# A new order of steps, with newly assigned buffers, for a gated linear attention and mixing kernel on one core

## The chip, the core and the metric

The kernel runs on one core of a Trainium2 chip. A core has five engines that each work through a list of instructions in order: TensorE (PE in the profile; its weight loads are PEld), VectorE (DVE), ScalarE (ACT), GpSimd (POOL) and SyncE (SP), which here issues all DMA transfers. They wait for each other by semaphores. The metric is the device time of one execution in microseconds (us).

## The reference, cut to what matters

```python
# q, k, v, f_logit: 4 batches, 8 heads, 768 tokens, 48 wide, fp32
f = sigmoid(f_logit)
for t in range(S):                      # per batch and head
    state = f[t][:, None] * state + outer(k[t], v[t])
    y[t] = q[t] @ state
x = y as (batch, token, 8 * 48 = 384)
theta = x @ w_theta                     # 384 x 384
zr, zi = x * cos(theta), x * sin(theta)
u = x + w_tok_r @ zr + w_tok_i @ zi     # 768 x 768 over tokens
out = u + relu(u @ w_ch)                # 384 x 384
```

## The kernel before

The tokens of a batch are cut into 6 chunks of 128; the four batches give chunks 0 to 23. For each chunk the attention part runs in chunk form, and then the mixing part. Half a batch (384 tokens) is a group; there are 8 groups, and each has 3 blocks of 128 channels. The work is written as steps with short names, and a table of strings, ORDER, lists 1169 steps; the main function walks through it, and each engine gets its instructions in that order. A suffix puts a step's operation on another engine (/A ACT, /D DVE, /P POOL). A second table, PLACES, says for each allocation of a buffer kind which of its buffers it takes. No scheduler changes the order afterwards: every engine works in order, so an instruction that waits holds all that stand behind it on its engine.

The steps of a chunk, in the order of their dependence, with the line on which their instructions are recorded:

- lf, lk, lq, lv: loads of f, k, q, v (SP, L560 and L565). lw: load of a part of a weight (L205). Each kind has 3 buffers per tag.
- gc (clamp, L272, DVE or POOL), go (two activations, L277 and L278, ACT), gs (scan over the tokens, L282, DVE), ge (p and f exponentials, L289 and L290, ACT), gq (q times p, L297, DVE or POOL), gk (k times f, L302, DVE), gp (copy of the chunk's last p into pes, L293, POOL). There is one buffer for p.
- ke (transposes of k into psk, L352, PE), kt (copy ktok out of psk, L179), up (state sums, L367, PE), sa (mid, L373 or L375, DVE), st (new state, L379, DVE), sm (its fading, L383, DVE or POOL).
- sc (scores, L338, PE), ma (mask, L344, DVE), qs (old state times q, L398, PE), ou (scores times v, L406, PE), xc (copy x out, L179), xt (transposes of x into pxt, L416, PE), xs (copy into ut, L179).
- th (angles, pth, L447, PE: from chunk 6 on in three products of an upper and a lower part, xh and xl), tn (rounding, L452 or L454), se (settle, L458, DVE), ab (fold, L463 on ACT or L465 on DVE), tr (two sines, L470 and L471, ACT), ro (x times sines gives z, L480, DVE), zh and zl (upper and lower part of z, L179 and L487).
- f0, f1, f2 (products over the tokens into pm, L503, PE: one step for each chunk of a group and each block of channels; for the first batch in full fp32, after it in three products of parts), v (adds pm to u, L507, DVE), uh and ul (parts of u, L179 and L514), c (channel product pch, L521, PE), cv (relu and sum, L535, DVE), so (store, SP).
- d1 to d5, e4, e5: the weights arrive as 64-bit words and are decoded on DVE (L218, L228, L229: raw, then value) and ACT (L223), and split into parts (L179, L253).

sc, up, qs and ou write into two double PSUM tiles, wide0 and wide1; psk, pxt, pth, pm and pch share four PSUM banks of the tag "b". ACT needs one table of functions for the gate's exponentials and logarithms and another for the sines; going from one to the other is an ACT_TABLE_LOAD.

Of the kernel before, what the change touches and what calls it, by code (L numbers as in the profile page):

```python
# [17 lines left out]
B, H, S, D = 4, 8, 768, 48  # L18
DM = H * D
P = 128  # L20
# [34 lines left out]


PLACES = {
    "a": "0110110101001010110101010101010101010101010101010",
    "b": ("012301230120123023300300002121123222230230203120310202001031023333312312023011203100000023"
        "1030303030032123123211120303031"),  # L60
    "f": "012012012012012012012012",
    "k": "012012012012012012012012",
    "q": "012012012012012012012012",
# [3 lines left out]
    "ut": "01201201",  # L67
    "v": "012012012012012012012012",
    "w": "010101010101010101010101",
    "wp": "0123456789abcdefghijklmno013245687cd",  # L70
    "x": "012012012012012012012012",
    "z": "0123450123412342342350421350421350421",
}
ORDER = (
# [37 lines left out]
)  # L112


# [636 lines left out]
```

## Time and profile before

| | us |
|---|---|
| three runs | 335.24, 335.41, 335.74 |
| their median | 335.41 |
| the profiled execution | 335.43 |
| its span from the first to the last instruction | 333.7 |
| PE busy | 319.3 (96%) |
| PE weight loads busy | 283.8 (85%) |
| DVE busy | 243.7 (73%) |
| ACT busy | 191.2 (57%) |
| POOL busy | 112.6 (34%) |

A profile gives for each instruction its engine, its line, when it began and how long it took. Matmuls overlap, so the time of one in a row of matmuls is longer than the distance between two starts; the distances are what adds up. An engine's idle time is put down to the instruction that released it. Of the chain of work that ended last, 89% lies on PE.

### The profile page before, as it was taken

What the parts mean: (1) busy time and instruction counts of PE and PEld (TensorE: products, weight loads), DVE (VectorE), ACT (ScalarE), POOL (GpSimd) and SP (SyncE); (2) the same over time, 40 slices, a digit from 0 to 9 for tenths busy, and PEclk for the clock granted to TensorE, in tenths of its full rate; (3) what the DMA queues carried; (4) which work ended last, traced back from release to release, by engine and by line L of the source; (5) the groups of instructions that cost most, each with busy time, mean ns of one, the idle gap of its engine ahead of it and who ended that gap; (6) DMA issues with size and microseconds to landing.
All of it is one profiled execution on the core that took longest, in us unless ns stands there. A gap on an engine that the chain in (4) does not pass through costs nothing.

```text
span 333.7 us, 10043 instructions
## 1 busy us (share of the span) xinstructions
PE 319.3 (96%) x4342; PEld 283.8 (85%) x4342; DVE 243.7 (73%) x397; ACT 191.2 (57%) x321; POOL 112.6 (34%) x109
## 2 busy tenths in 40 slices
PE   6599999999999999999999999999999999999992
PEld 6485667567676789999999999999999999999992
DVE  6999999999999899968659786764427677430031
ACT  6789977687696699847368254952806252300010
POOL 2452173318100146265371248153800521102110
PEclk9758999999999999999999999999999999999998
DMA  6988979858660464250404343250122102000022
GB/s 240 401 272 281 292 247 294 287 180 311 255 200 17 155 224 110 83 166 9 136 10 152 128 165 110 92 177 0 33 93 74 35 2 74 0 2 0 0 74 78
DMA packets 21619, 45.54 MB, mean 136 GB/s; under 512 B 2369, under 2 KB 5441, under 8 KB 21569
## 3 DMA queue, kind: packets, MB, share of 16 engines
q1 hardware_dynamic: 21568, 44.84, 40.6%
q8 instruction: 36, 0.59, 0.7%
q14 instruction: 15, 0.11, 0.1%
HBM read 40.11 MB, written 4.72 MB: 134 GB/s over the span
## 4 chain that ended last, share of the span: by engine, by line
PE 89%; DVE 3%; DMA 3%; ACT 2%; issue 1%; SPq 0%; DVEq 0%; ACTq 0%
PE pm L503 48%; PE pth L447 12%; PE pch L521 11%; PE wide L406 4%; PE wide L398 3%; PE wide L338 3%; PE pxt L416 3%; PE psk L352 3%; PE wide L367 2%; DMA q<-in_q_dram 2%; DVE f L282 1%; DMA f<-in_f_dram 1%; DVE q L297 0%; DVE k L302 0%; ACT L470 0%
## 5 line engine op out<-in xcount | busy, mean ns | idle before, releaser
L503 PE MATMUL pm<-wp,z 128*128 128x384 f32 x648 | 117.1, 336 | 0.0
L503 PEld LDWEIGHTS pm<-wp,z 128*128 128x128 f32 x648 | 112.4, 188 | 0.0
L503 PE MATMUL pm<-value,z 128*128 128x384 f32 x144 | 49.3, 488 | 0.4 <-DVE z L480 0.4
L503 PEld LDWEIGHTS pm<-value,z 128*128 128x128 f32 x144 | 26.3, 190 | 16.1 <-PE wide L406 0.5
L521 PE MATMUL pch<-uhl,wch 128*128 128x384 f32 x216 | 39.9, 338 | 0.0
L521 PEld LDWEIGHTS pch<-uhl,wch 128*128 128x128 f32 x216 | 37.5, 188 | 0.3
L507 DVE TENSOR_TENSOR ut<-pm,ut 128x384 f32<-128x384 f32 x24 | 13.1, 552 | 30.2 <-PE pm L503 30.2
L293 POOL COPY pes<-p 128x4 f32<-128x4 f32 x24 | 10.6, 440 | 71.0 <-ACT p L289 70.9
L179 ACT CAST uhl<-ut 128x384 fp32r<-128x384 f32 x18 | 9.2, 510 | 41.5 <-DVE ut L507 41.5
L282 DVE TENSOR_TENSOR_SCAN f<-carry,f 128x512 f32<-128x512 f32 x24 | 29.2, 1228 | 0.5 <-ACT f L278 0.5
L438 POOL TENSOR_TENSOR xl<-ut,xh 128x384 fp32r<-128x384 f32 x13 | 13.6, 1050 | 46.2 <-DVE xh L179 29.2
L289 ACT ACTIVATE p<-f 128x512 f32<-128x512 f32 x24 | 15.1, 628 | 22.3 <-DVE f L282 21.2
L514 POOL TENSOR_TENSOR uhl<-ut,uhl 128x384 fp32r<-128x384 f32 x13 | 13.5, 1046 | 37.0 <-DVE uhl L179 18.6
L272 POOL TENSOR_SCALAR f<-f 128x512 f32<-128x512 f32 x14 | 24.1, 1722 | 1.5 <-DMA f<-in_f_dram 1.5
L535 DVE SCALAR_TENSOR_TENSOR ut<-pch,ut 128x384 f32<-128x384 f32 x24 | 13.0, 552 | 14.6 <-PE pch L521 14.4
L447 PE MATMUL pth<-wth,xh 128*128 128x384 f32 x108 | 23.1, 348 | 0.0
L487 POOL TENSOR_TENSOR z<-w,z 128x768 fp32r<-128x768 f32 x9 | 16.8, 1863 | 17.1 <-ACT z L179 9.6
L406 PEld LDWEIGHTS wide<-v,sc 64*64 64x64 f32 x768 | 15.0, 140 | 8.8 <-DVE sc L344 3.6
L302 DVE SCALAR_TENSOR_TENSOR k<-f,k 128x512 f32<-128x512 f32 x24 | 19.3, 805 | 3.8 <-ACT f L290 3.8
L480 DVE TENSOR_TENSOR w<-w,x 128x768 f32<-128x768 f32 x18 | 18.2, 1013 | 4.0 <-ACT w L471 4.0
L458 DVE SCALAR_TENSOR_TENSOR w<-w,pth 128x384 f32<-128x384 f32 x24 | 13.2, 548 | 10.4 <-ACT w L452 10.3
L406 PE MATMUL wide<-v,sc 64*64 64x48 f32 x768 | 18.0, 231 | 2.3 <-DVE sc L344 2.3
(88 smaller groups left out, 609.1 us busy)
## 6 DMA issues: line engine op xcount, KB each, us to landing
v<-in_v_dram SPq DMA_DIRECT2D x24, 384.0 KB, 4.4
f<-in_f_dram SPq DMA_DIRECT2D x24, 256.0 KB, 4.1
k<-in_k_dram SPq DMA_DIRECT2D x24, 256.0 KB, 3.8
q<-in_q_dram SPq DMA_DIRECT2D x24, 256.0 KB, 3.9
raw<-in_w_r_dram SPq DMA_DIRECT2D x12, 384.0 KB, 4.8
raw<-in_w_i_dram SPq DMA_DIRECT2D x12, 384.0 KB, 5.4
out_dram<-ut SPq DMA_DIRECT2D x21, 192.0 KB, 1.9
raw<-in_w_theta_dram SPq DMA_DIRECT2D x3, 384.0 KB, 6.5
```

Of the source, the lines that this page charges most:

```text
L272: on(nc.vector).tensor_scalar(ft, ft, F_MIN, None, op0=ALU.max)
L282: nc.vector.tensor_tensor_scan(fl, carry[:, pairs(h)].rearrange("p n t -> p (n t)"), fl, 0.0, ALU.mult, ALU.add)
L289: nc.scalar.activation(ps_[m][:, pairs(h)], ft, AF.Exp, scale=-1.0)
L302: nc.vector.scalar_tensor_tensor(kt, loaded["f", m][:, pairs(h)], E_TOP, kt, op0=ALU.min, op1=ALU.mult)
L406: nc.tensor.matmul(out[HALF[t], j, p, :], scs[m][HALF[a], j, p, :], v2[HALF[a], t, p, :], start=(t == 0 and m % NC == 0 and p == 0), stop= ...
L438: on(nc.vector).tensor_tensor(xls[m], src, xhs[m], op=ALU.subtract)
L447: nc.tensor.matmul(pths[m], l, r, start=(n == 0), stop=(n == len(ms) - 1))
L480: nc.vector.tensor_tensor(zs[m] if full else w, w, xs[m].unsqueeze(1).to_broadcast([P, 2, DM]), op=ALU.mult)
L487: on(nc.vector).tensor_tensor(zs[m][:, 0], ws[m], zs[m][:, 1], op=ALU.subtract)
L503: nc.tensor.matmul(pms[g, d], l, r, start=(s == 0 and i == 0), stop=(s == NC - 1 and i == len(ms) - 1))
L514: on(nc.vector).tensor_tensor(us[g, d][:, 0], uts[g][:, d, :], us[g, d][:, 1], op=ALU.subtract)
L521: nc.tensor.matmul(pcs[g, d], l, r, start=(es[0] == 0 and n == 0), stop=(es[-1] == KD - 1 and n == len(ms) - 1))
```

## The change

The first 125 of the 1169 steps keep their order; all others come in a new one. Some steps move to another engine, and PLACES changes for the tags a (the double PSUM tiles), b (the PSUM banks), wp and z. No function is changed. Of the two tables this is the start of what changes:

```diff
-    "a": "0110110101001010110101010101010101010101010101010",
+    "a": "0110110011010101001001010101010101010101010101010",
-    "xt go d3 gs th lw gc ge gp tn se lv gq qs gk sc up ma lq d1 xs go gs sm/P ab/A th ge gq ke kt lk gp ou sa",
+    "xt go d3 gs th lw gc ge gp tn se lv gq qs gk sc up ma lq d1 xs go gs sm/P ab/A th ou ke ge tn sa xc d2",
```

By the tables, these numbers of steps move between engines: clamps gc on POOL 14 to 12, on DVE 10 to 12; gq on POOL 9 to 7; sm on POOL 11 to 16; copies kt on DVE 5 to 9; casts uh on DVE 6 to 13 and ul on POOL 13 to 9; zh on DVE 9 to 7; d5 on POOL 7 to 4. The switches of ACT's table, counted in the order, are 22 before and 26 now.

On PE, around the output step of chunk 7, where the attention steps of chunks 7 and 8 stand. In a row, the names give the tile with the number of its chunk or group, and the last columns the shape. Before:

```order
L503 MATMUL pm11_1139<-value9_1120,z0_624 128x384 x2
L352 MATMUL psk9_1173<-ident_70,k9_1022 128x112 x4
L406 MATMUL wide0_88<-v7_907,sc7_1178 64x48 x16
L338 MATMUL wide1_89<-q8_1010,k8_880 64x64 x16
L367 MATMUL wide1_89<-v9_1157,ktok9_1214 48x48 x16
L398 MATMUL wide0_88<-st7_1002,q8_1010 64x48 x2
```

Now:

```order
L503 MATMUL pm01_684<-value7_930,z4_1059 128x384 x2
L406 MATMUL wide1_89<-v7_780,sc7_1135 64x48 x16
L367 MATMUL wide0_88<-v8_1015,ktok8_1116 48x48 x16
L416 MATMUL pxt6_1183<-ident_70,x6_1048 128x128 x3
L503 MATMUL pm10_1187<-value8_990,z0_629 128x384 x2
L352 MATMUL psk9_1201<-ident_70,k9_1056 128x112 x4
L503 MATMUL pm10_1187<-value9_1052,z0_629 128x384 x2
L447 MATMUL pth6_1218<-wth1_85,xh6_1206 128x384 x3
L447 MATMUL pth6_1218<-wth0_84,xh6_1206 128x384 x3
L447 MATMUL pth6_1218<-wth1_85,xl6_1216 128x384 x3
L338 MATMUL wide0_88<-q8_1064,k8_883 64x64 x16
L398 MATMUL wide1_89<-st7_1045,q8_1064 64x48 x2
```

The output, scores, state and old-state steps stood in one block; now the output and a state step are one block, and the scores and the old state another, with transposes, products and angles between them.

On DVE, from the last common row (the scan of chunk 6) to the first z. Before:

```order
L282 SCALAR_TENSOR_TENSOR f6_392<-carry_67,f6_392 128x512
L297 TENSOR_TENSOR q5_504<-q5_504,p5_518 128x512
L375 TENSOR_TENSOR mid3_548<-wide0_88,st2_371 128x192
L379 TENSOR_TENSOR st3_550<-wide0_88,mid3_548 128x192
L383 TENSOR_TENSOR st3_550<-st3_550,pes_83 128x192
L302 SCALAR_TENSOR_TENSOR k5_529<-f5_300,k5_529 128x512
L228 SCALAR_TENSOR_TENSOR raw3_439<-raw3_439 128x768
L229 SCALAR_TENSOR_TENSOR value3_506<-raw3_439 128x768
L344 TENSOR_TENSOR sc3_620<-wide0_88,causal_75 128x512
L480 TENSOR_TENSOR z0_624<-w0_447,x0_282 128x768
```

Now:

```order
L282 SCALAR_TENSOR_TENSOR f6_392<-carry_67,f6_392 128x512
L375 TENSOR_TENSOR mid3_544<-wide0_88,st2_371 128x192
L458 SCALAR_TENSOR_TENSOR w1_542<-w1_542,pth1_514 128x384
L179 COPY ktok4_592<-psk4_534 128x384
L379 TENSOR_TENSOR st3_594<-wide0_88,mid3_544 128x192
L302 SCALAR_TENSOR_TENSOR k5_567<-f5_300,k5_567 128x512
L344 TENSOR_TENSOR sc3_622<-wide1_89,causal_75 128x512
L179 COPY ktok5_625<-psk5_617 64x384
L179 COPY ut0_390<-pxt2_613 128x3x128
L480 TENSOR_TENSOR z0_629<-w0_447,x0_282 128x768
```

The q scaling went to POOL, the decoding of value 3 behind z, and three copies and a settle step came in front of it.

On DVE, before the join that makes value 11. Before:

```order
L218 TENSOR_SCALAR raw12_1305<-raw12_1305 128x768
L302 SCALAR_TENSOR_TENSOR k10_1275<-f10_1056,k10_1275 128x512
L228 SCALAR_TENSOR_TENSOR raw11_1278<-raw11_1278 128x768
L229 SCALAR_TENSOR_TENSOR value11_1281<-raw11_1278 128x768
L282 SCALAR_TENSOR_TENSOR f11_1161<-carry_67,f11_1161 128x512
```

Now:

```order
L282 SCALAR_TENSOR_TENSOR f10_964<-carry_67,f10_964 128x512
L179 CAST uhl01_1291<-ut0_390 128x384
L218 TENSOR_SCALAR raw12_1212<-raw12_1212 128x768
L282 SCALAR_TENSOR_TENSOR f11_1120<-carry_67,f11_1120 128x512
L228 SCALAR_TENSOR_TENSOR raw11_1124<-raw11_1124 128x768
L229 SCALAR_TENSOR_TENSOR value11_1231<-raw11_1124 128x768
```

The scan of chunk 11 stood behind the join and now stands in front of it.

## Rows read from the trace of the kernel before

**Rows 1.** Stretches: from:to, length, busy time per engine (instructions), clock, DMA.
```profile
40.00:112.00 72.00, 71.97 (x1034) 48.91 (x1033) 70.43 (x109) 55.86 (x94) 23.33 (x21) 1.00 0.68 229
112.00:200.00 88.00, 87.97 (x1298) 84.77 (x1297) 71.73 (x119) 57.32 (x95) 39.52 (x33) 1.00 0.36 114
```

**Rows 2.** Waits of PE: engine, waiting line, released by, total, times, longest.
```profile
PE pxt L416 <- ACT x L179: 0.6, 1, 0.6
```

**Rows 3.** Timeline of PE: start, length, operation, count; angles, products, attention.
```profile
145.24 1.20 PE L447 MATMUL pth<-wth,xh 128*128 128x384 f32 x6
146.28 0.68 PE L447 MATMUL pth<-wth,xl 128*128 128x384 f32 x3
146.80 8.49 PE L503 MATMUL pm<-wp,z 128*128 128x384 f32 x48
...
260.33 1.20 PE L447 MATMUL pth<-wth,xh 128*128 128x384 f32 x6
...
261.98 0.72 PE L406 MATMUL wide<-v,sc 64*64 64x48 f32 x32
262.48 0.69 PE L338 MATMUL wide<-q,k 48*64 48x64 f32 x32
...
277.23 0.72 PE L406 MATMUL wide<-v,sc 64*64 64x48 f32 x32
277.88 1.31 PE L447 MATMUL pth<-wth,xh 128*128 128x384 f32 x6
```

**Rows 4.** Timeline of PE at a late angles step; chain of waits: start, length, what.
```profile
96.67 1.52 PE L447 MATMUL pth<-wth,xh 128*128 128x384 f32 x6
98.03 0.69 PE L447 MATMUL pth<-wth,xl 128*128 128x384 f32 x3
...
42.70 1.95 PE pth L447 x6
...
80.90 1.29 PE pm L503 x4
```

**Rows 5.** Timeline of DVE, 31 to 40 us, and of PE at the first products.
```profile
31.72 1.22 DVE L282 TENSOR_TENSOR_SCAN f<-carry,f 128x512 f32<-128x512 f32 x1
32.85 0.67 DVE L297 TENSOR_TENSOR q<-q,p 128x512 f32<-128x512 f32 x1
33.44 0.35 DVE L375 TENSOR_TENSOR mid<-wide,st 128x192 f32<-128x192 f32 x1
...
36.96 0.68 DVE L344 TENSOR_TENSOR sc<-wide,causal 128x512 f32<-128x512 f32 x1
37.76 0.96 DVE L480 TENSOR_TENSOR z<-w,x 128x768 f32<-128x768 f32 x1
...
38.87 1.53 PE L503 MATMUL pm<-value,z 128*128 128x384 f32 x4 [0.41 <-DVE z L480]
```

**Rows 6.** Groups by form: line, engine, operation, shapes, count, busy us, mean ns.
```profile
L179 DVE COPY ktok<-psk 128x384 f32<-128x384 f32 x4 | 2.2, 549 | 1.3 <-PE psk L352 1.3
L272 DVE TENSOR_SCALAR f<-f 128x512 f32<-128x512 f32 x10 | 4.2, 415 | 1.0 <-DMA f<-in_f_dram 1.0
L179 DVE CAST uhl<-ut 128x384 fp32r<-128x384 f32 x6 | 2.1, 353 | 0.0
L470 ACT ACT_TABLE_LOAD x11 | 14.1, 1283 | 0.2
L272 POOL TENSOR_SCALAR f<-f 128x512 f32<-128x512 f32 x14 | 24.1, 1722 | 1.5 <-DMA f<-in_f_dram 1.5
```

**Rows 7.** Timeline of PE and DVE at value 11, and PE's first channel step.
```profile
86.57 4.19 PE L503 MATMUL pm<-value,z 128*128 128x384 f32 x12
...
86.90 0.96 DVE L229 SCALAR_TENSOR_TENSOR value<-raw 128x768 int32<-128x768 int32 x1
...
111.48 1.85 PE L521 MATMUL pch<-uhl,wch 128*128 128x384 f32 x8
```

**Rows 8.** Operations on raw: count, shortest, median and longest ns, first and last.
```profile
L229 DVE SCALAR_TENSOR_TENSOR value<-raw x14: 558/959/1692, 14.5 to 96.7; 128x768 int32<-128x768 int32 x13, 128x384 int32<-128x384 int32 x1
```

More of the change, by code (lines that the diff above doesn't have):

```diff
@@ L57 @@
 PLACES = {
-    "a": "0110110101001010110101010101010101010101010101010",
-    "b": ("012301230120123023300300002121123222230230203120310202001031023333312312023011203100000023"
-        "1030303030032123123211120303031"),
+    "a": "0110110011010101001001010101010101010101010101010",
+    "b": ("012301230123021313133131120100131311201201021231321313132030120020001023012310120221122201"
+          "0310112122221231013010032103210"),
     "f": "012012012012012012012012",
@@ L69 @@
     "w": "010101010101010101010101",
-    "wp": "0123456789abcdefghijklmno013245687cd",
+    "wp": "0123456789abcdefghijklmno012354679bd",
     "x": "012012012012012012012012",
-    "z": "0123450123412342342350421350421350421",
+    "z": "0123450123401240140154032154032154032",
 }
```

66 rows, old and new, of the table ORDER are left out of this document.

## The prediction

> **What bounds the kernel now.** I first read the stretches with each engine's busy time [rows 1]. From 40 to 112 us TensorE (PE) is busy 71.97 of 72.00 us and VectorE (DVE) 70.43, so both are full; from 112 to 200 us PE still has 87.97 of 88.00, while DVE has fallen to 71.73 and ScalarE (ACT) to 57.32. The granted clock is 1.00 in both. PE is therefore the bound from about 40 us to the end, and up to about 112 us DVE, which makes most of PE's operands, is a second bound that runs level with it. A new order cannot change what PE computes: both orders hold the same PE steps. It can change three things: the time between two PE steps, the times at which PE waits, and the work left after the last matmul.
>
> The waits of PE that the profile names after the common start are short: 0.6 us for ACT's copy of x [rows 2] and 0.41 us for the first z [rows 5]. Less visible are three places where the angles' second half follows late: 98.03 - 96.67 = 1.36 us where the undisturbed run takes 146.28 - 145.24 = 1.04 us [rows 3, 4], so 0.3 us each. Together some 2 us in 300 can be won from waits, and no more than that.
>
> **The switch between matmul kinds.** The attention's four kinds (L338, L367, L398, L406) use 48 or 64 rows of the array, the others 112 or 128. The undisturbed nine matmuls of an angles step take 146.80 - 145.24 = 1.56 us to the start of a products step and 261.98 - 260.33 = 1.65 us to the start of an attention step: 0.09 us for going in. An L406 step takes 262.48 - 261.98 = 0.50 us to the next attention step and 277.88 - 277.23 = 0.65 us to an angles step: 0.15 us for coming out [rows 3]. So each block of attention steps costs 0.24 us, whatever its length. Counted in the PE order, the kernel before has 30 such blocks and the new one 35: the new order often cuts "ou sc up qs" in two or three (the first excerpt). That is 5 x 0.24 = 1.2 us on PE, which nothing covers, since PE is full. I take 1.2; a block that falls into one of PE's waits would cost nothing, so 0.7 to 1.2.
>
> **The start, 31 to 40 us.** PE's rows are the same up to the second angles step, DVE's up to the scan that starts at 31.72 and ends at 32.94 [rows 5]. Before, the q scaling (0.67) came next, then mid, and z began at 37.76, its table load and sines being late on ACT; the first products step began at 38.87 after an idle of 0.41. Now mid stands right behind the scan: done at 33.3, so the old-state step, which PE reaches at about 32.4, waits some 0.8 us there. After it I follow DVE's new rows (second excerpt) with the times of rows 5 and 6 (settle, ktok and ut take a ktok copy's 0.55, st is priced like mid, k like q): 0.55, 0.55, 0.35, 0.67, 0.68, 0.55, 0.55, and z 0.96, each some 0.08 less since they overlap. That puts ut at 36.8 and z at 37.7; the third angles step starts at 36.9, lasts 1.95 [rows 4], and the first products step starts at 38.9 with one more score step (0.5) behind it, thus about 0.4 us ahead of before. The table load now comes on ACT before the p and f exponentials, a gain for z, paid with another load right behind.
>
> **The stretch in which DVE feeds PE, 40 to 112 us.** The tight place of before is the join of value 11: DVE's L229 ends at 86.90 + 0.96 = 87.86, and PE's run of twelve records from 86.57 comes to it after four records of value 10, 1.29 us [rows 4], at 87.86 [rows 7]: no reserve at all. Against the common scan, DVE has in the new order, before that same join, two more ktok copies (2 x 0.55), a cast of uhl (0.35), three more clamps (3 x 0.415), one more scan (1.22), one more L454 (a PSUM operand of the same size as ktok's: 0.55) and one more fold (priced like mid, 0.35), together 4.8; and fewer: a q (0.67), a k (0.67), a mask (0.68) and three short operations of 192 columns (3 x 0.35), together 3.1 [rows 5, 6]. DVE has 1.7 us more to do. PE has before it one more products step (1.29 [rows 4]) and a block (0.24), less a key transpose and a state step (0.4 each, 86.57 and the run before): 0.7 us more. If DVE lost as much time in the new order as in the old, PE would come 1.0 us late there. What DVE lost: from 32.94 to 87.86 are 54.9 us, where its 81 operations, each at the median time from start to start of its form, add up to some 50.1, so 4.8 us, of which six operations account for 2.7 by taking far longer than their usual time (L229 up to 1.692 against 0.959 [rows 8]); the rest are its own waits. I take 0.7 less in the new order: 0.4 from the start, where z and the next mask no longer wait, and 0.3 because GpSimd (POOL) has there seven or eight long operations (clamps of 1.72 [rows 6] and q) instead of nine. This leaves 1.0 - 0.7 = +0.3 us. It swallows the 0.4 us of the start, which is inside it and not added. Bounds: -0.4 (DVE never late, PE keeps the gain of the start) to +2.0 (DVE loses 1.0 more than before).
>
> **The rest.** ACT has 26 table loads instead of 22 (11 of each kind), 4 x 1.283 = 5.1 us more [rows 6]; ACT is busy 55.86 of 72 us in the first stretch and 57.32 of 88 in the second [rows 1], and that room hides them. Without that cover a load would cost its 1.28 us. Operations moved from POOL to DVE late in the program (casts, splits) fall where DVE has 16 us free in 88: nothing. Loads on the DMA queue: I compared for each k and v the PE step that frees its buffer, with the stores queued ahead, and the PE step that uses it; the shortest distance is about 5 us before and 7 after by the step times above, so nothing either way. A PSUM bank is taken again one products or split step (six matmuls, 1.04 as in rows 3) after its last use at five places, before at one. The copy in between takes 0.55 [rows 6], so it fits if its engine is free; I take 0 and keep 0 to 1.5 us for the range. The end is alike: the last PE steps are six channel steps, then three additions and one store, and the splits that they need are made 1 us or more ahead.
>
> **The sum.** The profiled execution took 335.43 us, the median of the three runs is 335.41, so it stands for them. 335.43 + 1.2 + 0.3 = 336.9 us, 0.45% slower. A difference of 0.2%, 0.67 us, is about the least that a measurement of this kernel can tell from none.
>
> **Rivals.** (1) *PE keeps ahead of DVE's lateness.* If DVE is in time throughout, the start's gain of 0.4 stays: 335.43 + 1.2 - 0.4 = 336.2, with 0.7 for the blocks 335.7: within 0.2%, mostly. It speaks for it that DVE loses least where it begins without waits; against it, that the reserve of before was nil at value 11. (2) *The waits go and outweigh the blocks: faster.* All of the 0.6, the 0.41 and the three times 0.3 would be won, 1.9, and 0.4 at the start is partly the same; with blocks at 0.7 to 1.2 it gives 334.2 to 334.8. It decides from the point at which more than 1.9 us of waiting is gone. Its mechanism is that DVE is less often held up by POOL: the stretch's nine long POOL operations become seven or eight and stand elsewhere, so in the best case none of the six lengthened DVE operations (2.7 us) recurs. For it: L229's two lengths [rows 8]. Against: POOL is still full of work in the stretch, and before the common scan nothing changes. [...] (3) *Waits in order pile up later.* With PSUM banks taken again after 1.04 us and chains of copy, split and sine spread over engines that work in order, each late copy holds PE: some five to eight waits of 0.3 to 0.5 us more, 338.4 to 340. For it: five close reuses instead of one. Against it: after 112 us every engine but PE has room.
>
> **How the numbers follow.** Forecast as summed (336.2 to 338.2): 0.47. Rival 1, no change or just slower: 0.22. Rival 2, faster: 0.17. Rival 3: 0.14. The range should leave out about 2 in 10: the lower end takes in rival 1 and the edge of rival 2, 335.0; the upper end takes the bounds of DVE's lateness (1.2 + 2.0) and part of rival 3, 338.8. Faster by over 0.2%, below 334.7: 0.17. Within 0.2%, 334.7 to 336.1: 0.21. Slower, above 336.1: 0.62.
>
> **What would show it.** In the new profile, nine matmuls of angles to an attention step should again take 0.09 more, and leaving one 0.15 more, at 35 places. The first products step should start near 38.9 with the old-state step waiting for mid before it. At value 11 and at the first z of chunk 4 PE should wait for DVE, and the first channel step should start about 0.6 us earlier than the 111.48 of before [rows 7], with one products step less behind it, if I am right about DVE's pace; 1 us earlier or more means rival 1 or 2. After 112 us PE's waits should be as short as now; if they add up to over 1 us, rival 3. I am wrong altogether if DVE's lengthened operations vanish or double.

## The result, and the profile after

| | us | runs | ratio to the kernel before (95% interval) |
|---|---|---|---|
| before | 335.74 | 335.24 to 335.95, five | |
| after | 337.95 | 336.76 to 340.19, five | 1.0079 (1.0054 to 1.0105) |
| after, once more | 338.60 | 336.79 to 342.24, eight | 1.0092 (1.0058 to 1.0127) |

The new order is slower by 2.2 us. That is on the side I had forecast and inside my range, 1 us above the 336.9. But its runs lie over more than 3 us where those of before lie over 0.7, and no term of my sum spreads like that. The longest of the eight runs of the repetition is a slow one that its ratio leaves out. The profiled execution is the 340.19 one, so 4.8 us above the profiled one of before.

From its page, these are the busy line, the granted clock in 40 slices, and the head of the chain that ended last (before: PE 319.3, DVE 243.7, ACT 191.2, POOL 112.6):

```profile
PE 322.6 (95%) x4342; PEld 284.8 (84%) x4342; DVE 257.3 (76%) x411; ACT 194.1 (57%) x318; POOL 106.7 (32%) x102
...
PEclk9959899999999999999999999999999999999998
...
PE 77%; DVE 14%; issue 3%; DMA 3%; ACT 1%; SPq 0%; DVEq 0%; ACTq 0%
```

DVE has 13.6 us more to do and POOL 5.9 less, as the moved steps said. The new thing is "issue 3%" in the chain: time in which the engine waited for nothing that the profile shows. The waits of PE (engine and line, what it waited for, us in total, times, longest), over the whole span, say where; this answers [rows 2]:

```profile
PE wide L406 <- DVE sc L344: 2.9, 3, 2.0
PE wide L338 <- issue: 2.2, 1, 2.2
PE wide L398 <- DVE mid L375: 0.6, 1, 0.6
```

One wait of 2.2 us that no semaphore ends. PE's timeline (start, length, operation, count, idle before) around it, which answers the PE row of [rows 5]:

```profile
35.67 0.34 PE L338 MATMUL wide<-q,k 48*64 48x64 f32 x8
38.22 0.58 PE L338 MATMUL wide<-q,k 48*64 48x64 f32 x24 [2.20 <-issue]
38.73 3.53 PE L447 MATMUL pth<-value,ut 128*128 128x384 f32 x6
42.05 3.15 PE L503 MATMUL pm<-value,z 128*128 128x384 f32 x8
```

PE does 8 of the 32 matmuls of the scores of chunk 4, stands still for 2.2 us with 24 left that read the same q and k as the first 8, and goes on. The angles of chunk 2 behind take 3.32 us to the next start instead of about 2. Why, the stretches show (length; busy of PE, PEld, DVE, ACT, POOL with their counts; granted clock; DMA share; GB/s), as [rows 1] did for before:

```profile
31.30:39.40 8.10, 5.28 (x195) 4.30 (x188) 6.43 (x14) 6.64 (x10) 2.75 (x4) 1.00 0.94 304
39.40:42.90 3.50, 3.50 (x7) 1.89 (x6) 3.47 (x4) 0.59 (x2) 1.47 (x1) 0.51 1.01 361
42.90:112.00 69.10, 68.95 (x957) 45.62 (x956) 66.14 (x104) 56.43 (x91) 18.31 (x17) 1.00 0.61 199
```

From 39.4 us, 1.2 us after PE goes on, the granted clock is 0.51 for 3.5 us, and then 1.00 again. After that PE's busy time is as full as before. So most of the 4.5 us between the two spans comes from six microseconds near 38 us: 2.2 of idle time, and some 1.3 of slow clock. A further 0.6 us lies in waits of PE's weight loads, which the list of PE's waits leaves out; they come up in the account of the prediction.

### The profile page after: what moved, and what is told of

Its sections match the earlier page's. It is cut to its first block, busy times and chain, and to the rows that moved or that the text cites. A ratio compares the mean times of both kernels' runs of the same rounds, so it can differ in the third digit from the quotient of the medians.

```text
span 338.2 us, 10070 instructions
## 1 busy us (share of the span) xinstructions
PE 322.6 (95%) x4342; PEld 284.8 (84%) x4342; DVE 257.3 (76%) x411; ACT 194.1 (57%) x318; POOL 106.7 (32%) x102
## 4 chain that ended last, share of the span: by engine, by line
PE 77%; DVE 14%; issue 3%; DMA 3%; ACT 1%; SPq 0%; DVEq 0%; ACTq 0%
PE pm L503 41%; PE pch L521 11%; PE pth L447 10%; PE wide L406 3%; DVE f L282 3%; PE wide L398 3%; PE wide L338 3%; PE pxt L416 2%; DVE raw L228 2%; PE psk L352 2%; DMA raw<-in_w_i_dram 2%; PE wide L367 2%; DVE raw L218 1%; DVE q L297 1%; DVE value L229 1%
## 5 line engine op out<-in xcount | busy, mean ns | idle before, releaser
L503 PE MATMUL pm<-wp,z 128*128 128x384 f32 x648 | 119.2, 337 | 0.0
L503 PE MATMUL pm<-value,z 128*128 128x384 f32 x144 | 50.2, 492 | 0.1
L521 PE MATMUL pch<-uhl,wch 128*128 128x384 f32 x216 | 40.4, 339 | 0.0
L282 DVE TENSOR_TENSOR_SCAN f<-carry,f 128x512 f32<-128x512 f32 x24 | 31.2, 1301 | 0.9 <-ACT f L278 0.9
L487 POOL TENSOR_TENSOR z<-w,z 128x768 fp32r<-128x768 f32 x10 | 20.7, 2075 | 28.4 <-DVE z L179 18.5
L272 POOL TENSOR_SCALAR f<-f 128x512 f32<-128x512 f32 x12 | 20.9, 1748 | 24.3 <-DMA f<-in_f_dram 16.0
L383 POOL TENSOR_TENSOR st<-st,pes 128x192 f32<-128x192 f32 x16 | 12.5, 784 | 38.6 <-DVE st L379 32.9
L179 ACT CAST uhl<-ut 128x384 fp32r<-128x384 f32 x11 | 5.6, 511 | 32.7 <-DVE ut L507 32.7
L514 POOL TENSOR_TENSOR uhl<-ut,uhl 128x384 fp32r<-128x384 f32 x9 | 10.3, 1148 | 36.2 <-DVE uhl L179 21.9
L452 ACT ACTIVATE w<-pth 128x384 f32<-128x384 f32 x15 | 7.3, 489 | 23.2 <-PE pth L447 23.2
```

Source lines behind the costliest of these rows:

```text
L272: on(nc.vector).tensor_scalar(ft, ft, F_MIN, None, op0=ALU.max)
L282: nc.vector.tensor_tensor_scan(fl, carry[:, pairs(h)].rearrange("p n t -> p (n t)"), fl, 0.0, ALU.mult, ALU.add)
L487: on(nc.vector).tensor_tensor(zs[m][:, 0], ws[m], zs[m][:, 1], op=ALU.subtract)
L503: nc.tensor.matmul(pms[g, d], l, r, start=(s == 0 and i == 0), stop=(s == NC - 1 and i == len(ms) - 1))
L521: nc.tensor.matmul(pcs[g, d], l, r, start=(es[0] == 0 and n == 0), stop=(es[-1] == KD - 1 and n == len(ms) - 1))
```

## The experiments

Two theories to begin with. **Late instructions**: PE's own instructions are not there in time. **An accident, or a load**: something else held this one execution or these scores. Beside them the terms of my sum had to be measured, above all the switch between matmul kinds.

### Does it repeat, does it follow the step, do the loads make it?

> The changed kernel once more, nothing edited, to see what repeats. In the profiled execution of it TensorE stood still for 2.20 us in the middle of the scores of chunk 4 (after 8 of the 32 matmuls, at 36.0 us; the trace names no semaphore), and the angles of chunk 2 behind it then took 3.53 us where they take 2.1 at the high clock. Theory of late instructions (TensorE's own instructions had not yet been fetched, because the fetch came behind the loads of the data): a gap again at the same place, behind matmul 8 of these scores or nowhere, but of another length, and the spans of the executions differ by the length of the gap and of the slow clock behind it; an execution without the gap has a span near 338.2 - 2.2 - 1.4 = 334.6 us. Theory of an accident of that one execution: no gap, and the times lie together within 0.5 us near 338.

Measured: 338.60 us median. Its profiled execution (337.88, span 335.9) on PE:

```profile
36.17 0.34 PE L338 MATMUL wide<-q,k 48*64 48x64 f32 x8
37.81 0.58 PE L338 MATMUL wide<-q,k 48*64 48x64 f32 x24 [1.30 <-issue]
38.32 2.20 PE L447 MATMUL pth<-value,ut 128*128 128x384 f32 x6
40.36 2.74 PE L503 MATMUL pm<-value,z 128*128 128x384 f32 x8
```

The same gap behind the same matmul, 1.30 us long this time, and no slow clock behind it: it is 1.00 from 40 to 43 us, and the angles take 2.04 us. So it is no accident, and it is one source of the spread: the longer gap, 2.20 us, cost its own length and then 1.3 us of slow clock as well.

> The changed kernel with fewer bytes in flight when the gap arises: the loads of weight parts 5 and 6 (two transfers of 384 KB each, issued at 35.3 and 38.2 us) are issued behind the load of k of chunk 7 (at 39.6 us) instead, and the first decode step of part 5 goes behind them on VectorE. TensorE's order is as in the changed kernel. Late instructions behind loads: the gap at the scores of chunk 4 is gone or under 0.5 us, and the time is 336.3 to 336.9. Rival, the gap has nothing to do with the loads: it stays 1 to 2 us and the time near 338.

```diff
-    ... f1 d3 f0 lw xc/D se xt lf st qs tr xs ab up gk lv lw d1 ke ma tr lk gp ...
+    ... f1 d3 f0 xc/D se xt lf st qs tr xs ab up gk lv ke ma tr lk lw lw gp ...
```

Measured: 337.92 us (337.01 to 338.63, six runs), ratio 1.0059 (1.0039 to 1.0079). The gap stands at the same matmul and is 1.06 us long. Moving 1.5 MB of loads did not remove it, so this run spoke for the rival; at most, loads lengthen it. It is a weak test: in the changed kernel only half of these loads are issued before the gap, and without them the DMA share from 34 to 38 us still was 0.76 (0.91 in after_again).

> The changed kernel with one step moved on TensorE: the scores of chunk 4 go behind the angles of chunk 2 (2.1 us of matmuls) instead of ahead of them. Late instructions: the fetch that comes late is needed at the same count of TensorE's instructions (about 602 matmuls from the start), and with the long angles ahead of the short scores that count is reached some 2 us later, when the fetch has landed: no gap or one under 0.5 us, first products near 38.5 us, time 336.3 to 336.9. Rival, the scores of chunk 4 wait for something of their own that the trace does not name (a load of q or k): the gap of about 2 us stands at the scores again, wherever they are, and the time stays near 338.

```diff
-    ... ge ou lk lv sc ab th sa d1 tn lq
+    ... ge ou lk lv ab th sc sa d1 tn lq
```

Measured: 339.54 us (338.64 to 340.91, six runs), ratio 1.0120 (1.0099 to 1.0142): slower still. The gap is gone from the scores, as the first theory wants, but the gain did not come. VectorE's timeline tells why:

```profile
39.93 0.36 DVE L375 TENSOR_TENSOR mid<-wide,st 128x192 f32<-128x192 f32 x1 [1.88 <-PE wide L338]
...
43.48 0.55 DVE L179 COPY x<-wide 128x384 f32<-128x384 f32 x1
```

The middle state of chunk 4 (L375) reads the double PSUM tile into which these scores are written (in the new table both scores 3 and 4 have wide1), and in the order it stands behind them. So when the scores moved, DVE waited 1.88 us, the copy of x behind it came late, and PE waited 1.52 us before the transposes of x. The experiment had a side effect of its own. It showed the gap leaving this place, not what it costs.

### Can PE run out of instructions?

> A measurement, not a candidate: the kernel before, with the 32 matmuls of a scores step written 3, 5, 7 and 9 times in a row in chunks 16, 18, 20 and 22 (the same values again into the same tile, so nothing else changes; all in the stretch after 180 us, where few loads run). At the 15 ns from one small matmul to the next that the scores take, the 20 additional rounds are 20 x 0.48 = 9.6 us. Theory of late instructions (fetched in packets of 256 instructions, 128 matmuls with their weight loads, each usable 2.1 to 2.3 us after its packet starts, while 128 small matmuls need 1.9 us): no gap in chunk 16 or a short one, gaps without a semaphore in chunks 20 and 22 at intervals of 128 matmuls, each 0.3 to 2 us, in sum 2 to 8 us, so 347 to 353 us. Rival, small matmuls can run in any number one behind the other, and the gap in the changed kernel has another cause: no such gaps, 345.3 us.

```diff
-        for p in range(NP):
+        for p in list(range(NP)) * {16: 3, 18: 5, 20: 7, 22: 9}.get(m, 1):
```

Measured: 355.41 us (354.20 and 356.61), above the 353 that I had given at most; the 9.6 us of matmuls explain about half of the 18.5 to 20.9 us more. In the profiled execution PE stops four times without a semaphore, 5.0 us in all: 0.62 us behind the scores of chunk 16, 1.51 behind those of chunk 20, and twice in the scores of chunk 22, 288 matmuls in a row:

```profile
272.74 2.21 PE L338 MATMUL wide<-q,k 48*64 48x64 f32 x137
276.17 2.09 PE L338 MATMUL wide<-q,k 48*64 48x64 f32 x128 [1.21 <-issue]
279.89 0.52 PE L338 MATMUL wide<-q,k 48*64 48x64 f32 x20 [1.64 <-issue]
```

Between the gaps stand exactly 128 matmuls. With their weight loads these are 256 instructions, and one instruction packet on the queue q8 is 16 KB; if one packet holds them, these are 64 bytes for each. The page of the changed kernel has 36 such packets, which by this estimate have room for 9216 instructions, and PE's matmuls and weight loads there are 8684. In the profiled execution of the changed kernel, where PE stops at 36.0 us, one such packet begins after 35.9 us, and none in the microsecond before (queue, packets, MB, share of 16 engines, in the windows 34.9 to 35.9 and 35.9 to 37.0 us; the line of q1 is that of the loads):

```profile
q1 hardware_dynamic: 101, 0.20, 93.7%
...
q1 hardware_dynamic: 169, 0.42, 98.0%
q8 instruction: 1, 0.02, 5.3%
```

In the measurement, queue q1 has nothing from 272.7 to 280.5 us; the one line is

```profile
q8 instruction: 2, 0.03, 2.1%
```

These two packets lie at 273.5 and 277.2 us, and PE goes on at 276.17 and 279.89, some 2.6 us behind each. The stretches around the gaps read (columns as above):

```profile
272.00:276.00 4.00, 2.95 (x171) 2.64 (x170) 0.11 (x1) 1.09 (x3) 1.81 (x1) 1.00 0.02 4
276.00:280.00 4.00, 2.20 (x133) 2.06 (x136) 0.00 (x0) 0.00 (x0) 0.00 (x0) 1.00 0.02 4
280.00:284.00 4.00, 4.00 (x79) 3.91 (x79) 2.17 (x4) 0.48 (x1) 1.72 (x1) 0.57 0.01 4
```

From 276 to 280 us DVE, ACT and POOL do nothing, and the DMA share is 0.02: no load is in the way. At 15 ns each, 128 matmuls need 1.9 us, and PE went on only some 2.6 us after a packet began: they used up their instructions faster than these arrived. That it is the instructions that PE lacks is read from the packets and from the 128 between the gaps; the trace names nothing that it waits for. By this reading PE ran dry without any load, and this is against my own sentence: not "behind the loads", but too many short instructions in a row. In the changed kernel too PE goes on 2.3 to 2.4 us behind such a packet (I had put 2.1 to 2.3), at the same matmul in three profiled executions; how much the loads, which are dense there, add to it is not shown. In the changed kernel the output step of chunk 2, keys, old state, scores and state sums, transposes, keys, the output step of chunk 3 and the scores of chunk 4 follow each other with no long matmul in between, 171 matmuls and then 8; the order before has the 2 us of the angles ahead of the last output step. The kernel before, with 36 such packets too, has no such stop of PE from 25 us on; here two of them cost 1.21 and 1.64 us.

The third row of these stretches shows the second part of the price once more: behind the two gaps the clock falls to 0.57 on the mean of four microseconds, with the products running. This happened at 280 us, where the kernel before has 1.00. Behind the single stop of 1.51 us in chunk 20 it falls as well, to 0.61 on the mean of 244 to 247 us.

### The gap taken away

> The changed kernel with three steps moved: the scores of chunk 4 behind the angles of chunk 2 on TensorE, as in the run sc4_later; the middle state of chunk 4 on VectorE now stands ahead of these scores in the order, so that it no longer waits for them (in sc4_later that wait held VectorE for 1.88 us, and x of chunk 3 and its transposes behind it); and one products step of the fourth group goes ahead of the output step of chunk 14, because TensorE stood 0.5 to 0.8 us behind two close blocks of small matmuls there. Theory that TensorE's instructions are fetched too slowly for a long unbroken stretch of small matmuls (in all three executions with the gap it ended 2.1 to 2.3 us after a 16 KB instruction packet began, at the same matmul 602): no gap without a semaphore at either place, VectorE's wait for the scores gone, time 335.9 to 336.8, and a spread between executions of under 1.5 us (that of the changed kernel was 5.5). Rival, the gaps are only cover for VectorE's lateness: the gaps go, waits of the same size for VectorE stand behind them, time 337.5 to 338.5.

```diff
-    ... ge ou lk lv sc ab th sa d1 tn lq
+    ... ge ou lk lv ab th sa sc d1 tn lq
-    ... th f0 ul/P ou sm/P xc sc ul ... se xl f2 gq ge ...
+    ... th f0 ul/P f2 ou sm/P xc sc ul ... se xl gq ge ...
```

Measured: 337.07 us (335.54 to 338.48, twelve runs), ratio 1.0042 (1.0026 to 1.0057). The profiled execution (335.93, span 334.0) has no gap and no wait of DVE for the scores; all that PE's list of waits has from 25 us on is

```profile
PE pth L447 <- DVE ut L179: 0.4, 1, 0.4
PE wide L398 <- ACT x L179: 0.2, 1, 0.2
```

The mechanism did as expected; the median lies 0.3 us above what I had given, and the spread, 2.9 us, is twice what I had given. Two things changed at once here, and the runs do not price them apart. The moved products step has its own part: at the old-state step near 168 us three of the four profiled executions without it stop without a semaphore, after_again for 0.2 us, less_loads for 0.4 and sc4_later for 0.6, all three at the same matmul, and mended does not.

> The run mended once more, nothing edited, for a second profile: its profiled execution was at 335.93 us, the median at 337.07. If TensorE's own instructions are still late in the slower executions, this profile shows a gap without a semaphore in the angles of chunk 2 (matmul 602) or at another multiple of the packet, of 0.3 to 1.5 us, where the execution is above 336.5 us; if VectorE's waits or the clock at the start make the difference, there is no such gap.

Measured: 336.80 us, span 334.9, and again no gap. The 0.9 us between the two profiled executions are waits for DVE. Half of them are in PE's list, the largest the old-state step's; they bring the first products 0.46 us later:

```profile
PE wide L398 <- DVE mid L375: 0.6, 1, 0.6
PE pth L447 <- DVE ut L179: 0.4, 1, 0.4
```

The other half, again 0.46 us, is not in that list: PE's weight loads wait for a z and for value 11 (see below). So between these two executions it is not the fetch that differs but DVE, whose lateness, the wait for mid included, one of them has and the other has not.

> The run mended, with the angles of chunk 2 ahead of the output step of chunk 3 on TensorE (as the kernel before has it) and the copy of x of chunk 2 ahead of the mask of chunk 3 on VectorE, so that the angles need not wait. What mended left: the wait of the angles for that copy (0.37 us) and, in other executions of it, possibly a gap in the angles, which hold matmul 602 at 36.7 us while the packet was usable at 37.3 to 38.2 us in the three executions with the gap. Here matmul 602 comes in the output step behind 2.1 us of angles, at about 37.8 us. Theory of the fetch: first products at 38.3 to 38.5 us (39.1 in mended), no gap near 602, median 335.0 to 336.2, spread under 1.5 us. Rival, VectorE sets the pace there: the products start earlier, and later waits for VectorE give it back: median 336.7 to 337.3, as mended.

```diff
-    qs tr lk lw gq/P lf se sc kt/D st gk up xt ke ma gp kt/D sm/P xs/D ro ge ou lk lv sc ab th sa d1 tn lq
+    qs tr lk lw gq/P lf se sc kt/D st gk up xt ke xs/D ma gp kt/D sm/P ro ge th ou lk lv sa sc ab d1 tn lq
```

The products step of mended stands ahead of the output step of chunk 14 here too. Measured: 336.36 us (335.55 to 338.08, twelve runs), ratio 1.0019 (1.0000 to 1.0037). Its PE rows:

```profile
35.76 2.20 PE L447 MATMUL pth<-value,ut 128*128 128x384 f32 x6 [0.27 <-DVE ut L179]
37.89 0.72 PE L406 MATMUL wide<-v,sc 64*64 64x48 f32 x32
38.39 0.69 PE L338 MATMUL wide<-q,k 48*64 48x64 f32 x32
39.01 2.85 PE L503 MATMUL pm<-value,z 128*128 128x384 f32 x8
```

With the long angles ahead, all small matmuls run through, and the products start at 39.01 instead of 40.36 or 42.05. That is 0.5 us later than I had given, the median lies 0.2 us above my range, and the spread is 2.5 us, not under 1.5; the rival's 336.7 to 337.3 is missed too. Three microseconds of reordering near 36 us, and one products step, take the kernel from 2.2 us above the one before to 0.5 above the 335.82 that the one before took beside it, which the interval hardly tells from none. It is not a version that beats both.

### What a cut block costs

> The kernel before with nine of its blocks of attention steps on TensorE, all after 112 us, cut in two: a products step that stood behind the block goes between its scores and its state sums, nothing else changes, so that there are 39 blocks for 30. Theory of the switches (each entry into and exit from the small matmuls costs 0.09 + 0.15 us of TensorE's time): 9 x 0.24 = 2.2 us more, 337.6 us. Rival, the extra switches are hidden or cost nothing in sum: 335.4 to 335.8 us.

```diff
-    ... lf ul ro gc gs ou xc sc up tr qs sm/P xt f0 lk f0 go xs/D ...
+    ... lf ul ro gc gs ou xc sc f0 up tr qs sm/P xt lk f0 go xs/D ...
```

(one of nine). Measured: 342.02 us (341.58 to 342.81, five runs), ratio 1.0189 (1.0172 to 1.0206): 6.2 us, where I had given 2.2. One cut on PE, in the cut kernel:

```profile
184.96 0.72 PE L406 MATMUL wide<-v,sc 64*64 64x48 f32 x32 [0.46 <-DVE sc L344]
185.46 0.69 PE L338 MATMUL wide<-q,k 48*64 48x64 f32 x32
186.09 1.31 PE L503 MATMUL pm<-wp,z 128*128 128x384 f32 x6
187.33 0.51 PE L367 MATMUL wide<-v,ktok 64*48 64x48 f32 x13
```

and the same place in the kernel before:

```profile
181.54 0.69 PE L338 MATMUL wide<-q,k 48*64 48x64 f32 x32
182.02 0.57 PE L367 MATMUL wide<-v,ktok 64*48 64x48 f32 x16
```

Going out takes 186.09 - 185.46 = 0.63 instead of 0.48 us, 0.15 as I had read it. Going in takes 187.33 - 186.09 = 1.24 us for the products step instead of 1.04, so 0.20 and not 0.09: the 0.09 of [rows 3] is the price when an output step comes first, and here a state step does. That is 0.35 for a block, 3.1 for nine; all nine cuts read within 0.03 us of this (one of them lies at 106 us, not after 112). Another 2.3 us are waits of PE for DVE and ACT, six of 0.2 to 0.5 us after 112 us where the kernel before has none above 0.2, one of them in the first row above. The last 0.8 I did not place; in the profiled execution 0.5 us are there before the first cut, as the first products begin at 39.41.

> The run angles_first, with two of the blocks of attention steps that the change had cut joined again: the output step of chunk 12 and the scores of chunk 13 go behind the angles of chunk 11 to the state and old-state steps there, and the output step of chunk 20 goes to the scores of chunk 21; 33 blocks for 35. Theory of the switches: 0.24 to 0.34 us less for each, so 0.5 to 0.7 us less than angles_first. Rival, the joined blocks wait for a copy of x in the one PSUM tile between output and old state, and the gain goes: the same as angles_first or up to 0.3 us more. If both gains hold, this kernel lies below the kernel before (335.7): 334.4 to 335.5 us.

```diff
-    ... tn/D se ou sc ro xh ab/A ... d5 th xc qs up tn d5/P lf xt f1 se ... f1 f2 xs tr f0
+    ... tn/D se ro xh ab/A ... d5 th ou xc sc up qs tn d5/P lf f1 se ... f1 f2 xt xs tr f0
-    ... lq uh th ou xh ... th tr xc/D lv f1 kt/D ul gs sc qs tn up sm/P ...
+    ... lq uh th xh ... th tr lv f1 kt/D ul gs ou xc/D sc up qs tn sm/P ...
```

One place in the table of PSUM banks changes with it. Measured: 338.05 us (337.22 to 338.12, five runs), ratio 1.0056 (1.0037 to 1.0076): 1.7 us more than angles_first instead of 0.5 to 0.7 less. PE's waits from 34 us on:

```profile
PE wide L398 <- ACT x L179: 0.5, 1, 0.5
PE pch L521 <- DVE w L458: 0.5, 1, 0.5
PE wide L367 <- ACT ktok L179: 0.5, 1, 0.5
PE wide L338 <- DVE mid L375: 0.4, 1, 0.4
PE psk L352 <- DVE k L302: 0.2, 1, 0.2
```

2.1 us of waits, where angles_first has 0.5 in the same stretch. I had expected a wait at the joined blocks; most of these stand elsewhere (a channel step that the moved output step had covered, a state step that now waits for ktok in the queue of ACT). By the price above, joining a block saves PE about a third of a microsecond (this run does not show it by itself); the steps that it displaces cost more.

## Why the prediction was right, and where it was not

The forecast (slower, 336.9) and the range hold the result. By the steps of the working, however, one thing is missing from the sum, the stop of PE that I read as a wait for its own instructions (2.20 and 1.30 us), and one term, DVE's lateness, holds in some executions only. These are the marks that I had named, from the profiled executions (start in us):

| | first products | first channel step | last channel step | span |
|---|---|---|---|---|
| before | 38.87 | 111.5 | 327.5 | 333.7 |
| after | 42.05 | 114.2 | 332.0 | 338.2 |
| after, once more | 40.36 | 111.3 | 329.6 | 335.9 |
| mended | 39.09 | 110.2 | 327.9 | 334.0 |
| mended_again | 39.55 | 111.3 | 328.9 | 334.9 |
| angles_first | 39.01 | 110.1 | 327.7 | 334.0 |

- **The switches, +1.2 us: right in kind.** I had priced a block at 0.24 us; the cut blocks measure 0.35 when a state step comes first. Behind the first channel step the new order has three blocks and one products step more, 3 x 0.24 + 1.29 = 2.0 us by my prices. Measured from the first to the last channel step: 216.0 us before, 217.6 to 218.3 in the others, so 1.6 to 2.3 more. That part of the sum came out.
- **The start, -0.4 us: the waits as told, the end not.** The old-state step did wait for mid, 0.6 us instead of 0.8. I then followed DVE's rows and let PE's steps run as soon as their operands were there. I had taken it for granted that PE's instructions are. That is the step that failed: the changed order's first products came at 40.4 and 42.05 instead of 38.9. Without the gap they come at 39.0 to 39.6, each with the score step done.
- **DVE at value 11, +0.3 us: there in three profiled executions of the new order and its variants, not in the five others.** From 40 us on PE's list of waits names DVE in neither profile of the changed kernel, but it does not show everything. The weight loads (PEld) show more: in the profile after they wait 0.68 us for value 11. These are value 11's two decode operations in the profile after, the weight load that waits for them, and PE's sixteen products of this step; then the same decode operations and products in mended:

```profile
89.15 1.31 DVE L228 SCALAR_TENSOR_TENSOR raw<-raw 128x768 int32<-128x768 int32 x1
90.49 1.31 DVE L229 SCALAR_TENSOR_TENSOR value<-raw 128x768 int32<-128x768 int32 x1
91.86 0.94 PEld L503 LDWEIGHTS pm<-value,z 128*128 128x128 f32 x4 [0.68 <-DVE value L229]
87.76 5.66 PE L503 MATMUL pm<-value,z 128*128 128x384 f32 x16
...
84.42 0.93 DVE L228 SCALAR_TENSOR_TENSOR raw<-raw 128x768 int32<-128x768 int32 x1
85.39 1.25 DVE L229 SCALAR_TENSOR_TENSOR value<-raw 128x768 int32<-128x768 int32 x1
84.10 5.33 PE L503 MATMUL pm<-value,z 128*128 128x384 f32 x16
```

  To the next start the sixteen products take 5.59 us in the first and 5.26 in the second, so 0.33 us are lost at value 11. Some 20 us earlier the weight loads wait in the same way for the z of chunk 4, and 0.26 us are lost there. These are the two places that I had named. (The kernel before has such a wait too, of 0.49 us for value 11.) less_loads loses 0.29 and 0.33 us at them, mended_again 0.13 and 0.33; after_again, sc4_later, mended, angles_first and joined lose nothing. So PE keeps ahead, as in rival 1, or loses up to 0.6 us; my sum had 0.7 for it, from -0.4 to +0.3. Without the loss the first channel step begins at 110.1 to 110.2, where rival 1 gives 110.3: the start's 0.4, one products step of 1.29 less and two blocks of 0.24 more. In the three executions that lose time, GpSimd runs a clamp beside all of L228 and a fading and a copy beside L229, and each takes 1.31 us; in mended the clamp begins late in L228, which takes 0.93. DVE's operations thus did lengthen beside GpSimd's, as I had it. Which of the two ways an execution goes is open.
- **The late angles: misread.** I had counted three angles steps whose second half follows 0.3 us late [rows 4] as waits that could be won. Three rows of the kernel before show what they are:

```profile
80.74 1.46 PE L503 MATMUL pm<-value,z 128*128 128x384 f32 x4
81.73 1.51 PE L447 MATMUL pth<-wth,xh 128*128 128x384 f32 x6
83.08 0.69 PE L447 MATMUL pth<-wth,xl 128*128 128x384 f32 x3
```

  The full-precision products step ahead of them takes 0.99 us to the next start instead of 1.29, and the first six matmuls of the angles 1.35 instead of 1.04. The 0.3 us changes its row and is in no sum. Rival 2 had 0.9 us less to win than I gave it.
- **The rest, 0: right but for the gap.** The table loads, the POOL steps, the reused PSUM banks and the end show in no wait of PE above 0.2 us after 40 us; the 0.6 us for x of [rows 2] are gone. Rival 3, late copies that hold PE in many places, is not there; some runs reach its 338.4 to 340, but the one profiled above that, 340.19, has the gap instead.

The profiled executions can be added up from these terms. Without gap and without DVE's loss the sum is rival 1's, 335.43 + 1.2 - 0.4 = 336.2; angles_first took 335.92 and mended 335.93. The first profile of the changed kernel has DVE's loss of 0.6, the gap of 2.2 and 1.3 us of slow clock: 340.3, measured 340.19. The second has a gap of 1.3 alone: 337.5, measured 337.88. So the sign was earned by the switches, and the 336.9 is nearly the sum with DVE's loss and without the gap. That the median of 337.95 lies in the range, with a gap in both profiles that no term of the sum holds, is in part luck. What remains open: how often the runs without a profile have the gap, why PE went on later in the 340.19 execution (38.22 us) than in the one of 337.88 (37.81), and what the 0.8 us in before_cut is.

## What to carry to other kernels

In a kernel with very short matmuls, read the order for unbroken stretches of them, not only for operands: behind some 170 in a row without a long matmul PE stopped here for 1.06 to 2.20 us, and with the angles' 2.1 us ahead of the scores it did not. Such a stall carries no semaphore in the profile ("issue"), so a wait without a name in the middle of a group of equal instructions is the sign. Look at the weight loads' waits beside the matmuls': DVE's lateness at value 11 stood only there. And in a tuned order, count a moved step with everything that read its tile or stood behind it: two of my own repairs (sc4_later, joined) lost more to that than they won.

## What the runs showed of the hardware that I had not expected

- PE stopped where the profile shows nothing that it waits for, which I read as a wait for its own instructions. In a row of 288 matmuls of 15 ns it stopped twice, with 128 of them in between, for 1.21 and 1.64 us, with a DMA share of 0.02; in the changed kernel behind matmul 8 of the scores of chunk 4, for 2.20, 1.30 and 1.06 us in three profiled executions.
- An idle time of 2.2 us in a full stretch was followed by 3.5 us at a granted clock of 0.51; one of 1.3 us by none; one of 1.5 us by 0.61 on the mean of three microseconds; gaps of 1.2 and 1.6 us, 2 us apart, by a mean of 0.57 over 4 us. So such a stall cost more than its length in some of these cases. The changed kernel's runs lie between 336.8 and 342.2 us, those of the two orders whose profiles have no gap (mended, angles_first) between 335.5 and 338.5; less_loads, with a gap in its profile, spreads over only 1.6 us, so how much of a spread is the gap is not shown.
- The price of going from 128-row matmuls into the 48- or 64-row ones differed with the step that comes first: 0.09 us for an output step (before), 0.20 for a state step (before_cut).
